# Decode attention: the last value load in pieces of 64, 40 and 24 chunks, its first rows added by products with a 0/1 matrix

## The chip, the cores and the metric

The kernel runs on one core of one Trainium2 chip. The metric is device microseconds of one execution, lower is better. A profile of one execution gives times from the span's start, in microseconds.

## The reference

One decode step (one token, D = 512) of an attention block, gated by a small MLP block:

```
xn  = layernorm(x)
q   = (xn @ wq) as 32 heads of 128
K,V = the last 4096 rows of each head's cache (32 heads, 32768 x 128, bf16)
s   = softmax(q.K * 128**-0.5) . V   as one row of 4096, @ wo
g   = silu(_B_ref(xn))               # layernorm, gelu, two small linear layers
out = x + s * g
```

The sequence has length 1, so the shifts inside the MLP block leave only zeros in its first half. Keys and values of all heads are 67 MB; they are read once. With the weights 79 MB are loaded.

## The kernel before, in words

**Tiling.** The 32 heads go in NG = 8 groups of G = 4. `load_kv` brings the keys or values of a group as one tile of 128 partitions by CP = 128 chunks of 128 numbers: partition `32 a + b` holds 128 rows of head `a`. One tile is 4 MB. There are three key tiles and two value tiles in flight. All these loads, and the output, are issued on SyncE in program order (`load`).

**Loop.** Step `s` runs over NG + LAG = 10 steps: group `s` gets its scores, group `s-1` its softmax (`sm_...`), group `h = s-2` its product with the values. Inside this loop the order on TensorE, VectorE and ScalarE is the program's own (`tc.manual_schedule`). Scores of 64 or 80 chunks are made on VectorE (`k_vector`, L321 and L323), of the others on TensorE (`k_turn` L339, `k_scores` L350). `sm_exp` writes `pT`, the weights of each chunk for the 4 heads; `sm_den` (L394) and `sm_rden` make one over their sums.

**Values.** `v_wide` (L427) takes 4 chunks in one product: 16 columns of `pT` are the weights, 4 chunks of values (512 columns) move. The products go to four groups of 32 partitions of the accumulator `ov`, in turn. Row `32 r + 4 j + a` then holds, in its column block `j`, what belongs to head `a`; what stands in the other blocks is not wanted. So `ov` is copied to `ov_sb` (L433), turned by four transposes into `ot_ps` with an offset (`v_turn`, L444), and `v_add` (L450) sums the 16 wanted columns per 4 heads to `oT`. `v_out` (L471) multiplies by one over the sum and gives the 4 heads' columns `o`.

**The end.** The last group's values come in three pieces, `cuts = (0, 64, 96, CP)`: 64, 32 and 32 chunks. Behind them come the last four heads' rows of `wo` in two loads of two heads each (`load_rows`). In the last step the first two pieces are taken with `v_wide` (the second in 8 products), then turned and summed into `oT`; this `oT` lies in the accumulator memory, and `v_part` (L461) adds the last piece to it chunk by chunk, with the values as weights and 4 columns moving, so that no turn is needed. Between them stand the products of earlier heads with `wo` (`y_wide`, L518, copied to `y_sum` at L640, added by `rows_add`, L155). Then `v_out`, the four heads' rows (`y_head`, also L155), the product with `g_row` (L651), the sum with x (L653) and the store.

`warm` issues products whose result is not used. `ident_f` is a 128x128 identity in fp32; the pool `const` with the constants is allocated ahead of the pools of small tiles, weights and values.

Of the kernel before, what the change touches and what calls it, by code (L numbers as in the profile page):

```python
# [8 lines left out]
P = 128  # L9
BF16 = mybir.dt.bfloat16  # L10
FP32 = mybir.dt.float32
ACT = mybir.ActivationFunctionType
ALU = mybir.AluOpType
AX = mybir.AxisListType
# [4 lines left out]
G = 4  # L19
# [7 lines left out]
def kernel(  # L27
# [14 lines left out]
    nc = tc.nc  # L42
# [3 lines left out]
    _, H, Sk, Dh = A_k_cache.shape  # L46
# [5 lines left out]
    CP = G * W // P  # L52
# [10 lines left out]
    const = ctx.enter_context(tc.tile_pool(name="const", bufs=1))  # L63
    small = ctx.enter_context(tc.tile_pool(name="small", bufs=1))
    ps_misc = ctx.enter_context(tc.tile_pool(name="ps_misc", bufs=1, space=PSUM))
    ps_tr = ctx.enter_context(tc.tile_pool(name="ps_tr", bufs=3, space=PSUM))
# [3 lines left out]
    sm_pool = ctx.enter_context(tc.tile_pool(name="sm", bufs=3))  # L70
# [4 lines left out]
    def load(dst, src):  # L75
# [9 lines left out]
                        in_=A_wq.rearrange("(a b c) n -> b a (c n)", a=4, c=KC))  # L85
# [19 lines left out]
    ident_f = const.tile([P, P], FP32, name="ident_f")  # L105
# [16 lines left out]
    nc.vector.memset(neg_half[:], -0.5)  # L122

    masks = {}

# [24 lines left out]
    def rows_add(ps, col, w, last):  # L152
        k = col.shape[0]
        for j in range(KC):
            nc.tensor.matmul(ps[32 * j:32 * j + 1, :], lhsT=col, rhs=w[0:k, j * P:(j + 1) * P],  # L155
                             start=False, stop=last, skip_group_check=True)
# [46 lines left out]
    for b in range(2):  # L203
        zeros(qr[b][:])
        for c in range(KC):
            wc = wq_sb[:, c, :].rearrange("p (g a d) -> p g a d", a=G, d=Dh)
            for a in range(G):
                nc.tensor.matmul(qr[b][32 * a:32 * a + 1], lhsT=xq_bf[:, c:c + 1], rhs=wc[:, 4 * b:4 * b + 4, a, :],  # L208
                                 start=False, stop=(c == KC - 1), skip_group_check=True)
    nc.scalar.copy(out=q_row[:, 0:4, 0, :], in_=qr[0][:])  # L210
    nc.vector.tensor_copy(out=q_row[:, 4:8, 0, :], in_=qr[1][:])  # L211
    for b in range(2):
        qb_ps = ps_tr.tile([P, 4, Dh], FP32, tag="pt", name="qb_ps")
        nc.tensor.matmul(qb_ps[:], lhsT=sel[:].rearrange("k b a -> k (b a)"), rhs=q_row[:, 4 * b:4 * b + 4, 0, :],
                         start=True, stop=True)
        nc.scalar.copy(out=q_bc[:, 4 * b:4 * b + 4, :], in_=qb_ps[:])
    for b in range(2):
# [5 lines left out]
        for t in range(2):  # L223
            rows = slice(64 * t, 64 * t + 64)
            nc.scalar.copy(out=q_pair[rows, 4 * b:4 * b + 4, :, G * t:G * t + G].rearrange("p g l a -> p g a l"),
                           in_=qt_ps[rows].bitcast(BF16).rearrange("p g (a m l) -> p g a m l", a=G, l=2)[:, :, :, 0, :])
# [4 lines left out]
    for j in range(KC):  # L231
        for c in range(KC):
            nc.tensor.matmul(hs_ps[:, j:j + 1], lhsT=w2_sb[:, c, j::4],
                             rhs=shifted_bf[:, c:c + 1], start=(c == 0), stop=(c == KC - 1))
# [12 lines left out]
    for c in range(KC):  # L247
# [3 lines left out]
        for j, dst, w in parts:  # L251
            nc.tensor.matmul(dst, lhsT=z3_bf[:, c:c + 1], rhs=w, start=False, stop=(c == KC - 1),
                             skip_group_check=True)
# [14 lines left out]
    for i, (col, w) in enumerate(terms):  # L268
        r = 32 * (i % 4)
        nc.tensor.matmul(hr_ps[r:r + 1].rearrange("r j n -> r (j n)"), lhsT=col, rhs=w, start=False,  # L270
                         stop=(i >= len(terms) - 4), skip_group_check=True)
# [142 lines left out]
    def load_rows(h, n):  # L414
        load(wo_rows[:, h - h_part:h - h_part + n, :],
             A_wo[h * P:(h + n) * P, :].rearrange("(h p) n -> p h n", p=P))
# [6 lines left out]
    def v_wide(g, v, c1=CP, c0=0, last=True):  # L423
        s = st[g]
        for i in range(c0 // 4, c1 // 4):
            c, r = 4 * i, 32 * (i % 4)
            nc.tensor.matmul(ov[r:r + 4 * G], lhsT=s["pT"][:, c:c + 4, :].rearrange("p i a -> p (i a)"),  # L427
                             rhs=v[:, c:c + 4, :], start=(i < 4), stop=(last and i >= c1 // 4 - 4),
                             skip_group_check=True)
        if not last:  # L430
            return
        s["ov_sb"] = sm_pool.tile([P, 4, Dh], FP32, tag="ov_sb", bufs=2, name="ov_sb")
        nc.scalar.copy(out=s["ov_sb"][:], in_=ov[:])  # L433

    def v_turn(g):
        s = st[g]
        if g == NG - 1:
            ot_ps = ps_tr.tile([P, 4 * P], FP32, tag="pt", name="ot_ps")
        else:
            ot_ps = ps_misc.tile([P, 4 * P], FP32, tag="misc", name="ot_ps")  # L440
        s["ot"] = ot_ps
        step = P - 4
        for j in range(4):
            nc.tensor.transpose(ot_ps[:, step * j:step * j + P], s["ov_sb"][:, j, :], ident_f[:])  # L444

    def v_add(g):
        s = st[g]
        if g < NG - 1:
            s["oT"] = sm_pool.tile([P, G], FP32, tag="oT", name="oT")
        nc.vector.tensor_reduce(out=s["oT"][:], in_=s["ot"][:].rearrange("p (x m) -> p m x", m=32)[:, 0:G, :],  # L450
                                axis=AX.X, op=ALU.add)

    def v_open(g):
        st[g]["oT"] = ps_tr.tile([P, G], FP32, tag="pt", name="oT")
        nc.tensor.matmul(st[g]["oT"][:], lhsT=zero_bf[:], rhs=zero_bf[:, 0:G], start=True, stop=False,
                         skip_group_check=True)

    def v_part(g, v, c0, c1):
        s = st[g]
        for c in range(c0, c1):  # L460
            nc.tensor.matmul(s["oT"][:], lhsT=v[:, c, :], rhs=s["pT"][:, c, :], start=False,  # L461
                             stop=(c == CP - 1), skip_group_check=True)
# [60 lines left out]
        rows_add(y_ps, o_blk[3][:, h - h_part:h - h_part + 1], wo_row(h), h == H - 1)  # L523

    NG = H // G
    cuts = (0, 64, 96, CP)
    region = tc.manual_schedule(engines={mybir.EngineType.PE, mybir.EngineType.DVE,
                                         mybir.EngineType.Activation})
    region.__enter__()
# [1 line left out]
    for s in range(NG + LAG):  # L531
        h = s - LAG
        last = h == NG - 1
        kn = load_kv(k_pool, A_k_cache, s, (0, 64, CP) if s == 0 else (0, CP)) if s < NG else None
        if s == LAG:
            wts_guard.__exit__(None, None, None)
            v_pool = ctx.enter_context(tc.tile_pool(name="v", bufs=V_BUFS))
            wo_blk[2] = v_pool.tile([P, 4, D], BF16, tag="wo_4", bufs=1, name="wo_4")
            wo_rows = v_pool.tile([P, H - h_part, D], BF16, tag="wo_rows", bufs=1, name="wo_rows")
        if last:  # L540
            v = load_kv(v_pool, A_v_cache, h, cuts)
            for r in (H - G, H - 2):
                load_rows(r, 2)
        elif h >= 0:
            v = load_kv(v_pool, A_v_cache, h)
        if h == 3:
            wo_24 = k_pool.tile([P, 32, D], BF16, tag="kv", name="wo_24")
            wo_blk[0], wo_blk[1] = wo_24[:, 0:16, :], wo_24[:, 16:24, :]
            load_wo(0)
        if h == 5:  # L550
            load_wo(1)
            load_wo(2)

        if s < NG:
            nb = len(batches(s))

            def keys(b0, b1):
                for b in range(b0, b1):
                    k_turn(s, kn, b)
                    if b > 0:  # L560
                        k_scores(s, b - 1)

            k_open(s)
            k_vector(s, kn, 0)
            keys(0, 2)
            if s == 7:
                v_turn(h - 1)
                v_add(h - 1)
                v_out(h - 1)
            elif s > 1:  # L570
                sm_den(s - 2)
                sm_rden(s - 2)
            elif s == 1:
                sm_max(0)
            k_vector(s, kn, 1)
            keys(2, 4)
            if s == 7:
                sm_den(h)
                sm_rden(h)
                keys(4, nb - 2)  # L580
                sm_turn(s - 1)
                keys(nb - 2, nb)
            else:
                if s > 0:
                    sm_turn(s - 1)
                keys(4, nb)
            k_scores(s, nb - 1)
            sm_own(s)
            if s == 7:
                k_vector(s, kn, 2)  # L590
                v_wide(h, v)
                sm_exp(s - 1)
                v_turn(h)
                y_open()
                k_vector(s, kn, 3)
                v_add(h)
                v_out(h)
                ox_spread(1)
                sm_max(s)
                continue  # L600
            if s > 0:
                sm_exp(s - 1)
            if h > 0:
                v_turn(h - 1)
            k_vector(s, kn, 2)
            if h >= 0:
                v_wide(h, v)
            if h > 0:
                v_add(h - 1)
                v_out(h - 1)  # L610
            if s == 6:
                ox_spread(0)
            k_vector(s, kn, 3)
            if s == 6:
                ox_pick(0)
            if s > 0:
                sm_max(s)
        elif s == NG:
            ox_pick(1)
            sm_turn(NG - 1)  # L620
            sm_exp(NG - 1)
            y_wide(1, False)
            sm_den(NG - 2)
            sm_rden(NG - 2)
            y_wide(0, False)
            warm(3)
            v_wide(h, v)
            sm_den(NG - 1)
            sm_rden(NG - 1)
            v_turn(h)  # L630
            v_add(h)
            v_out(h)
            ox_spread(2)
        else:
            v_open(h)
            warm(3)
            v_wide(h, v, cuts[1], last=False)
            ox_pick(2)
            y_wide(2, True)
            nc.scalar.copy(out=y_sum[:], in_=yr[0][:].rearrange("p j n -> p (j n)"))  # L640
            v_wide(h, v, cuts[2], cuts[1])
            v_turn(h)
            v_add(h)
            rows_add(y_ps, ind, y_sum, False)
            v_part(h, v, cuts[2], CP)
            v_out(h)
            for r in range(H - G, H):
                y_head(r)
# [36 lines left out]
```

## Time and profile before

| | |
|---|---|
| median of 3 runs | 193.93 us (193.26 to 193.96) |
| span of the profiled execution, first to last instruction | 191.2 us |
| own time of the profiled execution | the page gives none beside the span; the median is 2.7 us longer than the span |
| busy: TensorE, VectorE, ScalarE | 116.4, 150.9, 89.2 us |
| DMA | 79.02 MB, mean 413 GB/s |
| mean granted TensorE clock | 0.720 |
| wo row loads: issue, to landing | 168.4 and 169.1 us, 18.5 us |

"Busy" counts instructions of an engine; the page cuts the span in 40 equal slices of 4.78 us and gives each engine's busy share in tenths (9 is 90% or more), the granted clock of TensorE, and what the DMA engines moved. A row of the timeline has start, duration, engine, line, operation, output and inputs, shapes and, in brackets, the idle time before it and what ended it. PEld is the loading of TensorE's weights.

### The profile page before, as it was taken

To read this page: it belongs to the slowest core of one execution; us is meant where nothing else is said; L and a number is where in the kernel's file an instruction comes from. 1 tells how busy PE (TensorE), PEld (TensorE's weight loads), DVE (VectorE), ACT (ScalarE), POOL (GpSimd) and SP (SyncE) were. 2 spreads that over 40 slices of the span, in tenths; PEclk is the share of its full clock that TensorE was granted. 3 is DMA by queue.
4 is the path that set the end of the run, shared out by engine and by line. 5 is a ranking of instruction groups with operands and counts; after the bars stand their busy time and mean duration, and the time that the engine had idled before them with its cause. 6 is when DMAs were issued, how large, how long until landed. Compare 5 with 4: busy or idle time off the path is not lost.

```text
span 191.2 us, 2839 instructions
## 1 busy us (share of the span) xinstructions
PE 116.4 (61%) x1159; PEld 74.2 (39%) x1159; DVE 150.9 (79%) x175; ACT 89.2 (47%) x191; POOL 2.3 (1%) x11
## 2 busy tenths in 40 slices
PE   1653754989825368256845772680888189739762
PEld 0430222767614334143334441540763077313322
DVE  1660159979999999999999999999999999980111
ACT  2001370888794076427464564542475148733120
POOL 2110000000000000000000000000000000000000
PEclk9999695555755557955695588557567858975998
DMA  6999999999999999999999999999999998999990
GB/s 211 447 430 404 431 418 439 439 439 437 432 434 439 432 429 432 432 439 432 422 432 432 418 422 418 452 439 435 439 432 434 435 432 372 471 425 405 420 371 32
DMA packets 4572, 79.02 MB, mean 413 GB/s; under 512 B 624, under 2 KB 1232, under 8 KB 1488
## 3 DMA queue, kind: packets, MB, share of 16 engines
q1 hardware_dynamic: 4264, 74.65, 91.6%
q10 hardware_dynamic: 296, 4.20, 5.1%
q8 instruction: 9, 0.15, 0.3%
q14 instruction: 3, 0.02, 0.0%
HBM read 78.84 MB, written 0.00 MB: 412 GB/s over the span
## 4 chain that ended last, share of the span: by engine, by line
DVE 46%; DMA 43%; PE 5%; ACT 3%; issue 1%; SPq 1%; ACTq 0%; DVEq 0%
DMA kv<-in_A_k_cache_dram 31%; DVE S L323 28%; DVE prod L321 15%; DMA kv<-in_A_v_cache_dram 10%; ACT kt L342 3%; DMA x_bf<-in_A_x_dram 2%; PE pt L339 2%; PE ov L427 1%; DVE m L366 1%; DVE S L364 1%; SPq L76 1%; PE sT L350 1%; DVE mx L374 1%; PE oT L461 1%; PE ot_ps L444 0%
## 5 line engine op out<-in xcount | busy, mean ns | idle before, releaser
L323 DVE TENSOR_REDUCE S<-prod 128x20 f32<-128x2560 bf16 (+1 forms) x32 | 86.0, 2686 | 1.1
L342 ACT COPY kt<-pt 128x1024 bf16<-128x1024 bf16 x52 | 51.2, 1013 | 40.4 <-PE pt L339 38.7
L339 PE MATMUL pt<-ident_f,kv 128*128 128x128 f32 x208 | 46.7, 376 | 10.8 <-DMA kv<-in_A_k_cache_dram 10.8
L321 DVE TENSOR_TENSOR prod<-kv,q_bc 128x2560 bf16<-128x2560 bf16 (+1 forms) x32 | 45.4, 1418 | 3.9 <-DMA kv<-in_A_k_cache_dram 3.7
L339 PEld LDWEIGHTS pt<-ident_f,kv 128*128 128x128 f32 x208 | 34.2, 196 | 14.4 <-DMA kv<-in_A_k_cache_dram 10.5
L350 PE MATMUL sT<-q_pair,kt 128*128 128x8 bf16 x416 | 19.4, 170 | 15.7 <-ACT kt L342 15.5
L350 PEld LDWEIGHTS <-kt 128*128 128x128 bf16 x416 | 16.4, 104 | 26.8 <-ACT kt L342 25.8
L427 PE MATMUL ov<-kv,pT 128*16 128x512 bf16 x248 | 22.0, 515 | 1.4 <-DMA kv<-in_A_v_cache_dram 1.4
L388 ACT ACTIVATE pT<-S,mb 128x128 bf16<-128x128 f32 x32 | 13.9, 573 | 0.3
L372 PE MATMUL mt_ps<-ident_f,m 128*1 128x128 f32 x8 | 2.9, 359 | 17.4 <-DVE rden L399 16.9
L433 ACT COPY ov_sb<-ov 128x512 f32<-128x512 f32 x8 | 4.7, 586 | 17.1 <-PE ov L427 17.1
L427 PEld LDWEIGHTS <-pT 128*16 128x16 bf16 x248 | 6.9, 109 | 13.2 <-issue 11.4
L359 ACT ACTIVATE own<-sT,par 128x48 f32<-128x48 f32 (+1 forms) x32 | 7.5, 356 | 3.7 <-PE sT L350 3.7
L444 PE MATMUL ot_ps<-ident_f,ov_sb 128*128 128x128 f32 x32 | 7.1, 359 | 2.9 <-ACT mb L384 1.9
L211 DVE CAST q_row<-qr_ps 128x512 bf16<-128x512 f32 x1 | 0.7, 692 | 9.9 <-PE qr_ps L208 9.9
L388 ACT ACTIVATION_READ_ACCUMULATOR pT<-S,mb 128x1 f32 x32 | 8.3, 258 | 0.0
L372 PEld LDWEIGHTS mt_ps<-ident_f,m 128*1 128x1 f32 x8 | 0.6, 80 | 17.9 <-DVE rden L399 17.2
L399 DVE RECIPROCAL rden<-den_ps 128x4 f32<-128x4 f32 x8 | 1.4, 175 | 7.0 <-PE den_ps L394 7.0
L381 PE MATMUL mb_ps<-md,par_t 5*128 5x4 f32 x16 | 3.9, 311 | 4.1 <-DVE md L376 4.1
L255 ACT ACTIVATE a_row<-a_ps 128x384 bf16<-128x384 f32 x1 | 0.5, 491 | 12.0 <-remote 12.0
L444 PEld LDWEIGHTS ot_ps<-ident_f,ov_sb 128*128 128x128 f32 x32 | 4.5, 178 | 3.9 <-ACT mb L384 2.3
L208 PE MATMUL qr_ps<-wq_sb,xq_bf 128*1 128x512 bf16 x32 | 3.1, 566 | 3.7 <-DMA wq_sb<-in_A_wq_dram 3.7
(122 smaller groups left out, 81.6 us busy)
## 6 DMA issues: line engine op xcount, KB each, us to landing
kv<-in_A_k_cache_dram SPq DMA_DIRECT2D x7, 4096.0 KB, 31.3
kv<-in_A_v_cache_dram SPq DMA_DIRECT2D x7, 4096.0 KB, 30.6
wq_sb<-in_A_wq_dram ACTq DMA_DIRECT2D x1, 4096.0 KB, 17.6
kv<-in_A_k_cache_dram SPq DMA_DIRECT2D x2, 2048.0 KB, 27.4
wo<-in_A_wo_dram SPq DMA_DIRECT2D x1, 2048.0 KB
kv<-in_A_v_cache_dram SPq DMA_DIRECT2D x1, 2048.0 KB
kv<-in_A_v_cache_dram SPq DMA_DIRECT2D x2, 1024.0 KB, 17.6
w_sb<-in_B_w_dram SPq DMA_DIRECT2D x1, 1376.0 KB, 9.1
```

The lines of the kernel that those rows point to most:

```text
L321: nc.vector.tensor_tensor(out=prod[:, 0:m, :], in0=kn[:, rows, :], in1=q_bc[:, g:g + 1, :].to_broadcast([P, m, Dh]), op=ALU.mult)
L323: nc.vector.tensor_reduce(out=st[g]["S"][:, rows], in_=prod[:, 0:m, :], axis=AX.X, op=ALU.add)
L339: nc.tensor.transpose(pt[:, i, :], kn[:, c:c + 2, :].rearrange("p c d -> p (c d)").bitcast(FP32), ident_f[:])
L342: nc.scalar.copy(out=kts[b][:, 0:n, :], in_=pt[:, 0:n, :].bitcast(BF16))
L350: nc.tensor.matmul(st[g]["sT"][:, c:c + 2, :].rearrange("p c a -> p (c a)"), lhsT=kt[:, i, l::2], rhs=q_pair[:, g, l, :], start=(l == 0), ...
L359: nc.scalar.mul(s["own"][:, 0:m, a], s["sT"][:, 0:m, a], par[:, a:a + 1])
L372: nc.tensor.transpose(mt_ps[:], s["m1"][:], ident_f[:])
L381: nc.tensor.matmul(mb_ps[:], lhsT=par_t[:].rearrange("k b a -> k (b a)"), rhs=md[:], start=True, stop=True)
L388: nc.scalar.activation(out=s["pT"][:, :, a], in_=s["S"][:], func=ACT.Exp, scale=scale, bias=mb[:, a:a + 1], accum_out=s["sum"][:, a:a + 1])
L427: nc.tensor.matmul(ov[r:r + 4 * G], lhsT=s["pT"][:, c:c + 4, :].rearrange("p i a -> p (i a)"), rhs=v[:, c:c + 4, :], start=(i < 4), stop=( ...
L433: nc.scalar.copy(out=s["ov_sb"][:], in_=ov[:])
L444: nc.tensor.transpose(ot_ps[:, step * j:step * j + P], s["ov_sb"][:, j, :], ident_f[:])
```

## The change

The last values are cut as 64, 40 and 24 chunks. The copy of `ov` for the last group is made in two halves, one on ScalarE and one on VectorE. Transposes and sum of the first two pieces give way to `v_fold`: four fp32 products with `ov_sb` as weights and a 0/1 matrix `fold` of 4 columns moving, added into the same `oT` as `v_part`; the `y_sum` products now stand ahead of it. `fold` is made once at the start from the identity, on VectorE, and takes 64 bytes per partition of the pool `const`. The last rows of `wo` come as three heads and one.

```diff
+    fold = const.tile([P, 4, G], FP32, name="fold")
+    nc.vector.tensor_reduce(out=fold[:].rearrange("p j a -> p (j a)"),
+                            in_=ident_f[:].rearrange("p (r m) -> p m r", m=32)[:, 0:4 * G, :],
+                            axis=AX.X, op=ALU.max)
...
         s["ov_sb"] = sm_pool.tile([P, 4, Dh], FP32, tag="ov_sb", bufs=2, name="ov_sb")
-        nc.scalar.copy(out=s["ov_sb"][:], in_=ov[:])
+        if g == NG - 1:
+            nc.scalar.copy(out=s["ov_sb"][:, 0:2, :], in_=ov[:, 0:2, :])
+            nc.vector.tensor_copy(out=s["ov_sb"][:, 2:4, :], in_=ov[:, 2:4, :])
+        else:
+            nc.scalar.copy(out=s["ov_sb"][:], in_=ov[:])
...
     def v_turn(g):
         s = st[g]
-        if g == NG - 1:
-            ot_ps = ps_tr.tile([P, 4 * P], FP32, tag="pt", name="ot_ps")
-        else:
-            ot_ps = ps_misc.tile([P, 4 * P], FP32, tag="misc", name="ot_ps")
+        ot_ps = ps_misc.tile([P, 4 * P], FP32, tag="misc", name="ot_ps")
...
-        if g < NG - 1:
-            s["oT"] = sm_pool.tile([P, G], FP32, tag="oT", name="oT")
+        s["oT"] = sm_pool.tile([P, G], FP32, tag="oT", name="oT")
...
+    def v_fold(g):
+        for j in range(4):
+            nc.tensor.matmul(st[g]["oT"][:], lhsT=st[g]["ov_sb"][:, j, :], rhs=fold[:, j, :], start=False,
+                             stop=False, skip_group_check=True)
...
-    cuts = (0, 64, 96, CP)
+    cuts = (0, 64, 104, CP)
...
-            for r in (H - G, H - 2):
-                load_rows(r, 2)
+            load_rows(H - G, 3)
+            load_rows(H - 1, 1)
...
             v_wide(h, v, cuts[2], cuts[1])
-            v_turn(h)
-            v_add(h)
             rows_add(y_ps, ind, y_sum, False)
+            v_fold(h)
             v_part(h, v, cuts[2], CP)
```

## The prediction

> **What bounds the kernel now.** I read the page first: the chain gives 43% to DMA and 46% to VectorE, so the slices decide between them.
>
> ```profile
> DVE  1660159979999999999999999999999999980111
> DMA  6999999999999999999999999999999998999990
> GB/s 211 447 430 404 431 418 439 439 439 437 432 434 439 432 429 432 432 439 432 422 432 432 418 422 418 452 439 435 439 432 434 435 432 372 471 425 405 420 371 32
> ```
>
> The DMA row is at 9 from the second slice to the last but one, at some 430 GB/s; VectorE is as busy only up to slice 36, and has little to do in the last 19 us. The transfers are the bound: what the engines do counts only if it delays an issue (none is near that: the last value pieces and rows are issued at 166.6 to 169.1 us and land some 17 to 19 us later, behind a queue) or if it comes after the last landing. So I read the end, in the chain of waits, in order of time:
>
> ```profile
> 167.79 18.54 DMA kv<-in_A_v_cache_dram
> 186.33 0.05 issue
> 186.38 0.97 PE oT L461 x32
> 187.35 0.02 issue
> 187.37 0.17 DVE o L471
> 187.55 0.04 issue
> 187.59 0.42 PE y_ps L155 x16
> 188.01 0.02 issue
> 188.04 0.30 DVE y L651
> ```
>
> The third value piece lands at 186.33; 32 products, one multiply and the 16 products of the four head rows follow it, to 188.01. The timeline shows what stands ahead of that on TensorE:
>
> ```profile
> 183.93 0.61 PE L427 MATMUL ov<-kv,pT 128*16 128x512 bf16 x8 [0.41 <-DMA kv<-in_A_v_cache_dram]
> 184.58 0.59 ACT L433 COPY ov_sb<-ov 128x512 f32<-128x512 f32 x1 [0.42 <-PE ov L427]
> 185.22 0.66 PE L444 MATMUL ot_ps<-ident_f,ov_sb 128*128 128x128 f32 x4 [0.69 <-ACT ov_sb L433]
> 185.81 0.40 PE L155 MATMUL y_ps<-y_sum,ind 128*1 128x128 f32 x8
> 185.91 0.23 DVE L450 TENSOR_REDUCE oT<-ot_ps 128x4 f32<-128x64 f32 x1 [2.83 <-PE ot_ps L444]
> 186.37 0.87 PEld L461 LDWEIGHTS <-kv 128*128 128x128 bf16 x32 [0.46 <-DMA kv<-in_A_v_cache_dram]
> ```
>
> Piece 2 is used from 183.93, and TensorE is done with it at 186.21, 0.16 us ahead of piece 3. There is a second end, in the answer on the tile wo_rows:
>
> ```profile
> L76 SPq DMA_DIRECT2D wo_rows<-in_A_wo_dram x2: 469/531/593, 168.4 to 169.1; - x2
> DMA to landing us min/median/max: 18.5/18.5/18.5
> ```
>
> The rows land at 186.9 and 187.6; the head products begin at 187.59 and show no stop. So two ends meet within 0.1 us: the work behind piece 3, and the last bytes.
>
> **The change, part by part**, on this execution's clock. Its span is 191.2 us; the median of the runs is 193.93, so 2.7 us lie around the span, and I add them unchanged.
>
> The pieces. Piece 2 grows by 8 chunks, 256 KB. The 1 MB of piece 3 now follows piece 2 by 2.44 us (183.93 to 186.37), so 256 KB are 0.61 us: TensorE gets piece 2 at 184.54. Piece 3 ends at the same byte, so it stays at 186.33. The same 4.5 MB follow in five loads on SP as before, behind at least 9 us of queued loads, so nothing is issued late. The rows split 3 and 1 have the same bytes: the last still lands at 187.6.
>
> Piece 2's wide products. 8 take 0.61 and 16 (181.50) take 1.04, so 0.054 for each further one; 10 take 0.72 and end at 185.26.
>
> The copy. ACT takes 0.59 for 512 columns and 0.17 for 4 (L384), so 0.38 for 256; VectorE takes 0.68 for 512 (L273) and 0.18 for a small one, so 0.42. Side by side they end at 185.26 + 0.04 + 0.42 = 185.72, and TensorE goes on at 185.77. Nothing waits behind the new VectorE copy but v_out, which comes 1.5 us later. The eight y_sum products (0.40) now run under the copies, to 185.66; y_sum is there from 184.16. Without that cover they would add up to 0.40.
>
> The fold takes the place of four transposes and the VectorE sum (185.22 to 186.14). No row has a product of this kind in a series. The nearest is L394: an fp32 product with 128 columns of weights and 4 columns moving is two loads and two matmuls.
>
> ```profile
> 178.40 0.30 PEld L394 LDWEIGHTS den_ps<-sum,ones_f 128*128 128x128 f32 x2 [0.43 <-issue]
> 178.40 0.39 PE L394 MATMUL den_ps<-sum,ones_f 128*128 128x4 f32 x2
> ```
>
> A load is 0.19 (shortest of four), two take 0.30, so one follows the other after 0.11. Four products are eight loads: the last begins at 185.77 + 0.77 = 186.54, and the first load of the next line at 186.65. Lower end: four loads spaced as the transposes' (0.42 for four), 0.09 each, done by 186.14, under the wait for piece 3. Upper end: four products with no overlap, 4 x 0.39 = 1.56, to 187.33. I take 0.11 a load, the row being the same instruction.
>
> Behind piece 3. 32 products take 0.97, the first 0.18, so 0.0255 for each further; 24 take 0.77. They begin at 186.65, held by the fold and no longer by the piece (0.28 late), and end at 187.42. From there to the first head product was 0.25 (187.34 to 187.59): 187.67. The last row (187.6, and 0.05 to react) is there. The 16 products end at 188.09 against 188.01: **+0.08 us**. The saved 0.20 of products and the 0.28 lost to the fold nearly cancel.
> With the ends of the fold: 187.33 + 0.77 + 0.25 + 0.42 = 188.77, +0.76; or, with the fold hidden, heads 28 to 30 from 187.39, then the wait for the last row to 187.65 and its four products (0.22 and three steps of 0.012): 187.91, -0.10.
>
> The new constant is one VectorE sum of 64 elements a partition; like sums take 0.15 (L120) to 0.37 (L296). At the start VectorE sits idle 3.38 us before L183, and 9.87 before L211 while the wq load comes; if it fell between two steps of the layernorm, it would be hidden by the wq load at 19.9.
>
> **The rivals.**
>
> Last row. If the fold costs less, the row that lands at 187.6 sets the end, 0.10 us earlier than now: 193.8. For it: the DMA row is full up to here. Against: eight fp32 loads must fit into 0.6 us.
>
> Slower: the clock falls. TensorE now idles 1.02 us (183.52 to 184.54) ahead of piece 2, where it was 0.41.
>
> ```profile
> 165.86:169.27 3.41, 1.83 (x19) 0.88 (x11) 3.38 (x3) 2.38 (x10) 0.00 (x0) 1.00 1.00 429
> 169.27:172.68 3.41, 1.50 (x12) 0.78 (x12) 2.04 (x10) 0.27 (x2) 0.00 (x0) 0.50 1.07 461
> 182.92:186.33 3.41, 1.98 (x24) 0.73 (x24) 0.39 (x2) 1.17 (x2) 0.00 (x0) 1.00 0.90 359
> ```
>
> (columns: length; PE, PEld, DVE, ACT, POOL busy; granted clock; DMA share; GB/s.) The clock fell to 0.50 behind a stretch with 1.83 us of PE busy, and stayed at 1.00 behind 1.98, so the point lies somewhere between. By my steps the last stretch has 0.39 + 0.72 + 0.40 + 0.56 = 2.07 after the change, which holds it; with other edges (180.5 to 183.9) it has 1.6, but so it has now. At half clock an L394 pair takes 0.50 and 0.59: 0.19 a load, so eight are 0.6 later; four L518 products take 0.60, so ten of piece 2 some 0.5 later; the heads 0.2 more (eight L155 products took 0.60 at 30.48, 0.40 here), the y_sum products 0.2: 1.5 in all, 195.5. It decides if the fall comes by 184.5; at 186.3 it costs 0.5.
> The Trainium skill ("TensorE: Matmul & The Clock Gate", Part 1 and the rules at the end) has the clock fall after an idle window of 3.4 us; with no gap over 1.02 us it would not fall here, but behind the first row above it fell with a longest gap of 1.9 us (168.1 to 170.0), so the trace does not bear the rule out.
>
> Slower: the addresses. The constant has 64 bytes a partition and stands ahead of the V and row tiles, which so far begin on a multiple of 256 bytes; they move to 64 past one. If their packets took 0.9% longer, the 45 MB outside the K tiles (105 us at 430 GB/s) would take 0.95 us more: 195.0. Against: the K tiles lie 128 past a multiple of 256, and the 32 KB packets of K and V loads both take 1.213 us at the median.
> The Trainium skill ("DMA: Bandwidth & Descriptors", How a descriptor splits into AXI transactions) charges a descriptor off a 256-byte edge extra beats, at most 8 in some 1024, an estimate of 0.8%; it says so of reads, and K against V does not show it.
>
> The change could also do nothing, if all transfers came earlier than its work; that is within the forecast.
>
> **How the numbers follow.** A measurement of this kernel tells about 0.5%, 0.97 us, from no change (the runs span 0.36%). Forecast, +0.08: 0.55. Last row, -0.10: 0.20. Both are within 0.5%, so 0.75. Clock: 0.10; addresses: 0.07; these are slower by over 0.5%, 0.17. Faster by over 0.5%: 0.08, for a cause that I do not see: the 16 engines do not finish together (DMA share 0.90 in the last stretch above), and a better balance would bring the rows earlier, but the fold would then hold the end. The time is 193.93 + 0.08 = 194.0. The range: down to 193.2, just under the fastest run; up to 195.0, which takes in +0.76 and the addresses, and leaves out the full fall of the clock and the unseen gain.
>
> **What would show it.** Right: piece 2's first product near 184.5, the fold's eight loads over some 0.8 us, the first L461-type load waiting for TensorE and not for DMA, the heads' end within 0.2 us of 188.0, the DMA row unchanged. Wrong: a stop at the last head (last row); PEclk under 1 from slice 39 on (clock); GB/s lower in all slices (addresses); any change ahead of 180 us, since by this working nothing there moves.

## The result, and the profile after

The changed kernel takes 194.02 us (median of 14 runs, 193.58 to 195.34), the kernel before 193.37 us (14 runs, 193.20 to 193.96). The ratio is 1.0039, with a 95% interval of 1.0021 to 1.0058: slower by 0.65 us. The forecast was 194.0 and "within 0.5%", which the ratio meets, though its interval reaches 0.58%; but the forecast's reason, +0.08 us at the end of the chain, is an eighth of what is there.

Of the page of the changed kernel, first the slices:

```profile
PEclk9999588555855555855795597555576855555897
DMA  6999999999999999999999999999999998999990
GB/s 192 443 431 418 414 434 437 437 437 439 427 432 437 430 427 437 437 430 423 427 416 423 423 433 423 444 437 427 437 437 432 434 437 372 468 420 403 419 362 28
```

The DMA row is as full as before, VectorE's share is the same (79% of the span), and a slice is too coarse to show a loss of 0.4%. PEclk, the granted clock, has more fives than before (22 for 17); that comes up below. The answer on the tile wo_rows shows more:

```profile
L76 SPq DMA_DIRECT2D wo_rows<-in_A_wo_dram x2: 486/540/593, 172.4 to 173.0; - x2
DMA to landing us min/median/max: 15.5/15.7/15.8
```

The last row lands at 173.0 + 15.5 = 188.5 us; before it was 187.6. No step of the forecast's chain moves that point, since the bytes are the same. The end of the chain, in order of time, with the `issue` entries of 0.02 to 0.04 us between the steps left out:

```profile
185.32 0.67 PE ov L432 x10
186.01 0.40 PE y_ps L160 x8
186.45 1.07 PE oT L465 x8
187.52 0.62 PE oT L471 x24
188.16 0.17 DVE o L481
188.37 0.47 PE y_ps L160 x16
188.86 0.30 DVE y L660
```

The DMA entry ahead of the last products has gone: by the profile the chain runs through TensorE. Yet piece 2, issued at 170.7, landed 14.4 us later, at 185.13, just ahead of its first product (185.17, first row below): a landing and TensorE's own work meet there. And the four heads' products take 0.47 from 188.37, where they took 0.42: the last head's row (188.5) comes just behind the first head's start. The two ends still meet, 0.9 us later than before. The timeline shows the new steps:

```profile
185.17 0.82 PE L432 MATMUL ov<-kv,pT 128*16 128x512 bf16 x10
186.02 0.37 ACT L439 COPY ov_sb<-ov 128x256 f32<-128x256 f32 x1
186.43 0.42 DVE L440 COPY ov_sb<-ov 128x256 f32<-128x256 f32 x1 [1.55 <-ACT ov_sb L439]
186.45 1.07 PE L465 MATMUL oT<-fold,ov_sb 128*128 128x4 f32 x8
187.37 0.74 PE L471 MATMUL oT<-pT,kv 128*128 128x4 bf16 x24
```

The halves of the copy do not run side by side: VectorE's waits for ScalarE's (the bracket), though no data pass between them. The fold starts behind ScalarE's half all the same.

### The profile page after: what moved, and what is told of

It is laid out like the page before. It is cut to its first block, busy times and chain, and to the rows that moved or that the text cites. A ratio compares the mean times of both kernels' runs of the same rounds, so it can differ in the third digit from the quotient of the medians.

```text
span 192.0 us, 2836 instructions
## 1 busy us (share of the span) xinstructions
PE 123.0 (64%) x1157; PEld 78.1 (41%) x1157; DVE 151.5 (79%) x176; ACT 89.2 (46%) x191; POOL 2.3 (1%) x11
## 4 chain that ended last, share of the span: by engine, by line
DVE 47%; DMA 33%; PE 15%; ACT 2%; issue 1%; SPq 0%; DVEq 0%; ACTq 0%
DMA kv<-in_A_k_cache_dram 31%; DVE S L328 28%; DVE prod L326 15%; PE ov L432 4%; PE pt L344 3%; DMA x_bf<-in_A_x_dram 2%; PE yr_ps L528 2%; PE ot_ps L450 1%; ACT kt L347 1%; PE sT L355 1%; PE wm L517 1%; DVE S L369 1%; DVE m L371 1%; DVE mx L379 1%; ACT ov_sb L442 1%
## 5 line engine op out<-in xcount | busy, mean ns | idle before, releaser
L344 PE MATMUL pt<-ident_f,kv 128*128 128x128 f32 x208 | 49.1, 391 | 10.6 <-DMA kv<-in_A_k_cache_dram 10.6
L344 PEld LDWEIGHTS pt<-ident_f,kv 128*128 128x128 f32 x208 | 36.0, 204 | 14.1 <-DMA kv<-in_A_k_cache_dram 10.2
L432 PE MATMUL ov<-kv,pT 128*16 128x512 bf16 x250 | 24.6, 558 | 0.0
L442 ACT COPY ov_sb<-ov 128x512 f32<-128x512 f32 x7 | 4.1, 587 | 19.2 <-PE ov L432 19.2
L432 PEld LDWEIGHTS <-pT 128*16 128x16 bf16 x250 | 7.1, 115 | 13.5 <-issue 12.3
L377 PEld LDWEIGHTS mt_ps<-ident_f,m 128*1 128x1 f32 x8 | 0.6, 80 | 17.8 <-DVE rden L404 17.2
L213 PE MATMUL qr_ps<-wq_sb,xq_bf 128*1 128x512 bf16 x32 | 3.6, 627 | 4.1 <-DMA wq_sb<-in_A_wq_dram 4.1
L386 PEld LDWEIGHTS mb_ps<-md,par_t 5*128 5x128 f32 x16 | 3.6, 276 | 5.8 <-PE sT L355 4.0
```

The source lines that it names most:

```text
L344: nc.tensor.transpose(pt[:, i, :], kn[:, c:c + 2, :].rearrange("p c d -> p (c d)").bitcast(FP32), ident_f[:])
L386: nc.tensor.matmul(mb_ps[:], lhsT=par_t[:].rearrange("k b a -> k (b a)"), rhs=md[:], start=True, stop=True)
```

## The experiments

Four causes were to be told apart: the fold (the forecast's), the pieces and rows, the clock, and the addresses, the rival with the smallest chance: the new constant moves the V tiles, and the row tiles beside them, from a multiple of 256 bytes to 64 past one. All were timed beside the kernel before. "Around" is the mean of time less span; "last row" is its landing in the profile.

| kernel | V tiles past 256 | ratio to before (95%) | median, us | median span, us | around, us | last row, us |
|---|---|---|---|---|---|---|
| before | 0 | 1 | 193.37 to 193.47 | 191.2 to 191.3 | 2.16 to 2.19 | 187.6 |
| the change | 64 | 1.0039 (1.0021 to 1.0058) | 194.02 | 192.25 | 1.80 | 188.5 |
| e1_gap64 | 64 | 1.0038 (1.0026 to 1.0051) | 194.31 | 192.1 | 2.17 | 188.6 |
| e2_after_pad128 | 0 | 0.9993 (0.9972 to 1.0015) | 193.21 | 191.45 | 1.81 | 187.4 |
| e3_fold_alone | 0 | 0.9972 (0.9961 to 0.9984) | 193.04 | 191.25 | 1.83 | 187.6 |
| e4_cuts_rows | 0 | 1.0005 (0.9994 to 1.0016) | 193.64 | 191.5 | 2.17 | 187.7 |
| e5_v64 | 64 | 1.0031 (1.0020 to 1.0042) | 194.06 | 191.9 | 2.18 | 188.4 |
| e6_small64 | 0 | 0.9996 (0.9987 to 1.0006) | 193.39 | 191.2 | 2.17 | 187.5 |
| e7_v128 | 128 | 1.0033 (1.0020 to 1.0046) | 194.03 | 191.9 | 2.17 | 188.5 |
| e8_const_alone | 0 | 0.9977 (0.9967 to 0.9987) | 193.06 | 191.2 | 1.82 | 187.5 |
| e9_k256 | 0 | 1.0002 (0.9978 to 1.0025) | 193.27 | 191.1 | 2.16 | |
| e10_fold_k256 | 0 | 0.9984 (0.9970 to 0.9998) | 192.84 | 191.0 | 1.82 | 187.4 |
| e11_fold_cuts | 0 | 0.9982 (0.9974 to 0.9991) | 193.04 | 191.2 | 1.83 | 187.6 |
| e12_memset | 0 | 0.9983 (0.9974 to 0.9993) | 193.16 | 191.3 | 1.85 | 187.8 |

No last row is given for e9_k256: in its profiled execution the transfers went at 394 GB/s from 21 to 48 us, where the kernel before had 429, and no line of it is used.

**e1_gap64: 64 unused bytes.**

```diff
     nc.vector.memset(neg_half[:], -0.5)
+    const.tile([P, 4, G], FP32, name="gap")
```

> The kernel before with an unused constant of 64 bytes a partition where the changed kernel has its 0/1 matrix; no instruction differs. It moves the V and row tiles from a multiple of 256 bytes to 64 past one. Addresses: the 32 KB packets of V loads take about 1.218 us instead of 1.213, all transfers end 0.3 to 0.7 us later, ratio 1.0015 to 1.004. Fold (the forecast's theory) and clock: nothing in it changes, ratio within 0.001 of 1.

Measured: 1.0038. Not one instruction differs, and the whole loss of the change is there. The answer on wo_rows, and the end of the chain:

```profile
L76 SPq DMA_DIRECT2D wo_rows<-in_A_wo_dram x2: 469/531/593, 168.8 to 169.5; - x2
DMA to landing us min/median/max: 18.9/19.0/19.1
```

```profile
168.21 18.87 DMA kv<-in_A_v_cache_dram
...
187.13 1.03 PE oT L462 x32
...
188.39 0.63 PE y_ps L156 x16
```

The third piece lands at 187.08 instead of 186.33, the last row at 188.5 to 188.6, and the products of the last two heads begin at 188.59, just behind it. That the 16 products take 0.63 for 0.42 is in part the clock, which was at 0.50 from 186.7 on in this execution; in e5_v64 (below), where it was at 1.00 from 179 to 189, the first two heads begin at 188.20 and the last two at 188.47, behind the row at 188.4. Engines, copies and products are those of before. The fold theory predicted no change here, so the fold does not make this loss.

**e2_after_pad128: the change, with V back on 256.**

```diff
-    small.tile([P, 96], BF16, name="pad")
+    small.tile([P, 64], BF16, name="pad")
```

> The changed kernel with its spare tile cut from 192 to 128 bytes, so that V and row tiles lie on a multiple of 256 bytes again, as before. Addresses: the loss is gone, ratio 0.999 to 1.001. Fold: the same loss as the changed kernel, ratio 1.002 to 1.006, with the fold ending after the third piece's landing. Clock: the same spread of times as the changed kernel, up to 195.3 us.

Measured: 0.9993, no loss; the median falls from the change's 194.02 to 193.21. Two of its twelve runs took 194.66 and 195.00 us, so the interval is wide; a spread like this was expected under the clock, and these two runs have no profile that could settle what makes it. Its chain, in an execution of 192.86 us, is the one that the forecast described (only the first `issue` entry is shown):

```profile
184.23 0.04 issue
184.27 0.83 PE ov L432 x10
185.13 0.38 ACT ov_sb L439
185.55 1.07 PE oT L465 x8
186.62 0.62 PE oT L471 x24
187.26 0.17 DVE o L481
187.48 0.42 PE y_ps L160 x16
```

Piece 2 lands at 184.23 and is taken at once; the fold, not a landing, releases the last 24 products.

**e3_fold_alone and e4_cuts_rows: the two halves of the change**, both with V on 256. The first is e2_after_pad128 with the old pieces and rows:

```diff
-    cuts = (0, 64, 104, CP)
+    cuts = (0, 64, 96, CP)
...
-            load_rows(H - G, 3)
-            load_rows(H - 1, 1)
+            for r in (H - G, H - 2):
+                load_rows(r, 2)
```

The second is the kernel before with these lines the other way round.

> The fold and the halved copy alone, with pieces of 64, 32 and 32 chunks, rows as two and two, V and row tiles on a multiple of 256 bytes. The fold's eight loads now start 0.6 us earlier (185.2 on the profile's clock) and end at 186.2, as piece 3 lands. Fold: no loss, ratio 0.999 to 1.001, and 32 products behind piece 3. If the fold is not the cause but the pieces are, likewise 1.000. If the fold's products lower the clock: over 1.002.

> The pieces of 64, 40 and 24 chunks and the rows as three and one alone, with the whole copy on ScalarE, four transposes and the sum as before, no new constant. By the rows of before: piece 2 at 184.54, 10 products to 185.26, copy to 185.9, transposes to 186.6, sum to 186.85, then 24 products to 187.55, heads from 187.8: 0.2 us later than before. Fold: ratio 1.000 to 1.002, no more than the changed kernel. Pieces: if the longer wait ahead of piece 2 lowers the clock, over 1.003 with times spread up to 195.

Measured: 0.9972 and 1.0005. Pieces and rows alone cannot be told from nothing (the median is 0.2 us later, as was expected from the rows of before, but the interval takes in no difference). The fold alone is faster, which no theory had expected; its span (191.25) is that of before, and of the 0.42 us that it gains, 0.33 lie around the span. That became a question of its own (e8_const_alone).

**e5_v64 and e6_small64: which tiles?** The new 64 bytes move the small tiles as well as the V tiles. The first moves the V and row tiles alone:

```diff
             v_pool = ctx.enter_context(tc.tile_pool(name="v", bufs=V_BUFS))
+            v_pool.tile([P, 32], BF16, tag="gap", bufs=1, name="gap")
```

The second has the constant of e1_gap64 and, behind the small tiles, 192 bytes more:

```diff
+    sm_pool.tile([P, 96], BF16, tag="gap2", bufs=1, name="gap2")
```

> The kernel before with 64 unused bytes at the head of the value pool alone: value tiles and the rows of wo that lie with them begin 64 bytes past a multiple of 256, all else stays where it was. If the transfers into the shifted value tiles are what the first experiment slowed: ratio 1.002 to 1.0045, the last row lands 0.5 to 0.9 us later than the 187.6 of before. If it was the small tiles (what engines read and write): 1.000.

> The kernel before with 64 unused bytes in the constants and 192 behind the small tiles: the small tiles lie 64 bytes further, the value tiles 256 bytes further and so again on a multiple of 256. Transfers theory: 0.999 to 1.001. Small tiles theory: the 1.0038 of the first experiment.

Measured: 1.0031 and 0.9996. The answers on wo_rows, of e5_v64 and then of e6_small64:

```profile
L76 SPq DMA_DIRECT2D wo_rows<-in_A_wo_dram x2: 471/966/1460, 168.7 to 170.2; - x2
DMA to landing us min/median/max: 18.2/18.5/18.9
```

```profile
L77 SPq DMA_DIRECT2D wo_rows<-in_A_wo_dram x2: 469/530/592, 169.6 to 170.3; - x2
DMA to landing us min/median/max: 17.1/17.2/17.2
```

170.2 + 18.2 = 188.4, and 170.3 + 17.1 or 17.2 = 187.4 to 187.5. The loss goes with the place of the V and row tiles, not with what the engines read and write. It builds up along the stream: the last value load of 4 MB lands at 176.4 to 176.5 us with V on 256 (before, e2, e6) and at 177.0 to 177.2 with V off it (the change, e1, e5, e7), so some 0.65 us of the 0.9 are there before the last pieces.

The packet records show it, too: behind 59 us a packet of 32 KB takes 1.2157 to 1.2158 us on the mean with V on 256 (before, e2, e3, e6) and 1.2189 to 1.2193 with V off it (the change, e1, e5, e7), 0.27% more; a 1 KB packet of the rows 46.0 and 47.1 to 47.7 ns. But it is not the value loads alone that slow down. With the packets ordered by start, 128 to a load, those of the key loads of groups 3 to 5 (counted from 0) take 1.214 us on the mean before and 1.217 in e1_gap64 and e5_v64, where no key tile moved; those of the value loads of groups 4 and 5 take 1.213, and 1.216 to 1.217. In e1, e5 and e7 the packets that each of the 16 DMA engines handles add up to more than before by some 0.3 us for the 112 of 32 KB of keys and values, 0.11 for those of 8 KB and 0.05 for the rows. That is about half of the 0.9 us; the rest lies in what the records do not tell apart.

**e7_v128: is 128 enough?**

```diff
+    const.tile([P, 8, G], FP32, name="gap")
```

> The kernel before with 128 unused bytes in the constants: value tiles begin 128 past a multiple of 256, where the key tiles lie in all kernels so far. If any offset from 256 costs: 1.002 to 1.0045, as at 64. If 128 is as good as 256 (as the equal packets of key and value loads in the kernel before suggest): 0.999 to 1.001.

Measured: 1.0033, as at 64. The argument that the forecast held against the addresses, that key tiles lie at 128 and do not suffer, was no guide to the V tiles. Offsets other than 64 and 128 were not tried.

**e8_const_alone and e12_memset: the time around the span.** The first makes the 0/1 matrix and does not use it (the spare tile cut as in e2_after_pad128). The second:

```diff
-    nc.vector.memset(neg_half[:], -0.5)
+    nc.vector.memset(neg_half[:, 0:1], -0.5)
+    nc.vector.memset(neg_half[:, 1:33], -0.5)
```

> The kernel before with the 0/1 matrix made at the start on VectorE and not used, the spare tile cut so that everything else stays where it was. By the forecast it costs nothing: span as before, 0.999 to 1.001. The three kernels with fold so far spend some 0.35 us less around the span than before; if the early instruction alone does that, 0.998; if it is the products or the halved copy, 1.000.

> The kernel before with the fill of one constant split in two on VectorE: one more instruction there, nothing else. If one more early VectorE instruction is what takes 0.35 us off the time around the span: 0.998, span as before. If it is the 0/1 matrix's own instruction: 1.000.

Measured: 0.9977 and 0.9983, with the span of before. The time around the span splits all kernels in two: 1.80 to 1.85 us in the seven with one more early instruction on VectorE (it runs at 7.7 us in e8_const_alone, at 1.2 us in e12_memset), 2.16 to 2.19 in the others, whatever else they do. That an early fill does the same as the 0/1 matrix shows that it is not the fold. What happens there is outside the profile, and stays open; whether a later instruction would do it was not tried.

**e9_k256 and e10_fold_k256: the key tiles on 256 too**, in the kernel before and with the fold, the spare tile 64 elements longer to keep V on 256:

```diff
+    head = ctx.enter_context(tc.tile_pool(name="head", bufs=1))
+    head.tile([P, 64], BF16, name="gap")
     k_pool = ctx.enter_context(tc.tile_pool(name="k", bufs=K_BUFS))
```

> The kernel before with 128 unused bytes ahead of the key tiles and as many more behind, so that key and value tiles both begin on a multiple of 256 (the key tiles lay 128 past one in all kernels so far). If each load of 4 MB into a tile off 256 loses what the value loads lose: 0.996 to 0.998, last row landing near 187.0. If key packets lose nothing there, as their medians of 1.213 us in the kernel before say: 0.999 to 1.001.

> The fold with the old pieces and rows, key and value tiles on a multiple of 256: the kernel meant to beat both. If key tiles matter: 0.993 to 0.996. If not: the 0.997 of the fold alone.

Measured: 1.0002 and 0.9984; against e3_fold_alone (0.9972) nothing is gained that can be told. While the V tiles lie on 256, key tiles at 128 cost at most 0.2%; V tiles at 128 cost 0.33%. In every slow kernel here the key tiles are off 256 as well; whether V tiles off 256 would also cost beside key tiles on it was not tried, and why the two differ is open. Two runs of e9_k256 took 195.72 and 196.02 us; it has neither fold nor new pieces, so times of this size come without them, and the profile of the one at 196.02 shows the slower transfers named under the table.

**e11_fold_cuts: fold and pieces, without the rows** (`cuts = (0, 64, 104, CP)` in e3_fold_alone).

> The fold with pieces of 64, 40 and 24 chunks, rows as two and two, value tiles on a multiple of 256. By the forecast's sum the later second piece makes the fold end after the third lands: 0.1 to 0.2 us over the fold alone, ratio 0.9975 to 0.999. If rows three and one are what costs: as the fold alone, 0.997.

Measured: 0.9982, with the span of e8_const_alone and e12_memset. The later second piece costs nothing that can be told. The two kernels that also split the rows as three and one on 256 (e2, e4) have spans 0.2 us longer; their intervals take in no difference, so this is a hint only.

Five kernels are faster than both the kernel before and the change (e3, e8, e10, e11, e12), by 0.16 to 0.28% against before. Since e8 and e12 have nothing but the extra instruction, that is what the others owe it to as far as the intervals can tell; the fold itself neither gains nor loses in the span.

## Why the prediction was right, and its reason wrong

**The time was met by luck, and the class by two errors that offset in part.** 194.0 was 193.93 + 0.08; 193.93 was the median of three runs and lies 0.56 us above the 193.37 of fourteen. The step itself was forecast as +0.08 and measured as +0.65. On medians it is made of span +0.95 us (191.3, in the runs beside e1_gap64, to 192.25) and around the span -0.36 us. Of the span's part e1_gap64 shows 0.8 us for the addresses; what is left for fold, pieces and rows is 0.15 (e2_after_pad128 against before), where the forecast had 0.08; the interval of e2_after_pad128, some 0.4 us either way, cannot tell these apart.

**The step that failed is the weighing of the addresses.** The mechanism was named, and its price, 0.95 us, is near what the last row shows (0.9). That the two agree is luck again: the price took packets to be 0.9% longer, and they came out 0.27% longer. The mechanism was given a chance of 0.07, and what was held against it was that key and value packets take the same time. That comparison could not show the cost. In the kernel before they do take the same time, but with the value tiles off 256 the key loads slow down as well (1.217 us a packet for 1.214): how fast a load into a key tile at 128 runs depends on where the value tiles lie. The sign "any change ahead of 180 us" came true (the last value load of 4 MB landed at 177.1 us in the change for 176.5); "GB/s lower in all slices" is too small to be seen in slices.

The Trainium skill ("DMA: Bandwidth & Descriptors", How a descriptor splits into AXI transactions) charges reads that start off 256 bytes; here the source is the same and only the place in the tile moved. The direction agrees, and 0.27% a packet lies under the prediction's estimate of at most 0.8%; but it is the same at 64 and at 128 bytes, and it falls on key loads whose tiles did not move, so no run here shows that rule to be the cause. What makes the packets longer stays open.

**The step left out: the time around the span.** "I add them unchanged" was wrong by 0.36 us. It was also mis-sized: 2.7 us was the median of three runs less another run's span, and pairs of the same run give 2.16.

**The chain at the end, term by term** (e2_after_pad128, relative to piece 3's landing at 186.06): piece 2 lands 1.83 us ahead, 1.8 forecast for its first product. Ten wide products take 0.83, 0.72 forecast. From their end to the fold 0.45, 0.51 forecast: the halves of the copy do not overlap, but the fold's first products need only ScalarE's half, so the error cost nothing. From the fold's first load to the end of the 24 products 1.69 (1.07 and 0.62), 1.65 forecast (0.88 and 0.77), so the row of L394 was a good guide. The heads start 1.42 behind piece 3, against 1.26 before: +0.16, +0.08 forecast. That the fold, not the piece, is what they wait for was right.

**The last row as the end** was right as a place, in the change (its last head waits 0.05 us), but late and not early: the row came 0.9 us later than the forecast took as fixed.

**The clock** was not the cause of the loss: e1_gap64 has the products of before and the whole loss, and e5_v64 has it with the granted clock at 1.00 from 179 to 189 us. The reading "the point lies somewhere between" 1.83 and 1.98 us of PE busy does not hold as a rule of busy time alone:

```profile
151.00:179.00 28.00, 22.15 (x174) 13.84 (x175) 20.28 (x28) 13.30 (x31) 0.00 (x0) 0.51 0.98 419
```

In the change's profile the clock stood at half for 28 us with PE busy for 79% of them (columns as in the prediction), 2.7 us in every 3.41. At half clock a product takes longer (one of L432 0.63 us for 0.38), so this busy time is not like that of the prediction's rows, and what sets the clock stays open. In this execution TensorE took piece 1 at 183.29, though its 16 products were not waiting for a transfer by then; at piece 2 (185.17) this delay and the later landing meet, so this profile alone cannot tell the two apart. The clock can hold the end of one execution: in the profile of e4_cuts_rows it is at 0.50 from 151.5 to 178.8 us, and the heads begin at 188.32 though the last row landed at 187.7; that execution took 194.06 us, the median of its kernel is 193.64. Whether the clock makes the three runs of the change above 195 us is not shown.

## What to carry to other kernels

Where the transfers are the bound, an added constant is not free just because it is small: it moves every tile allocated behind it. Before an edit is credited or blamed, run the kernel before with the same bytes added and nothing else, and read the landing of the last transfer, which showed 0.9 us here when the busy rows showed nothing. Below half a percent, compare the time around the span too.

## What the runs showed of the hardware that was not expected

- Value and row tiles that begin 64 or 128 bytes past a multiple of 256 in each partition cost 0.31 to 0.38% of a kernel that loads 79 MB at some 430 GB/s (e1, e5, e7); key tiles 128 past one cost nothing measurable while the value tiles lay on one (e9). With the value tiles off it, packets of the key loads took 1.217 us for 1.214, though the key tiles had not moved.
- One more early VectorE instruction, of 0.06 to 0.27 us, took 0.33 to 0.37 us off the time around the span, in the seven kernels of seven that have one; in two of them (e8, e12) nothing else that runs differs.
- TensorE's granted clock was 0.51 on the mean over 28 us in which PE was busy for 22.15 us.
